# Re-timing the first microseconds of an attention and MoE kernel: a planner's figures, k's cast ahead of q's, longer fillers, and another place for one group of transposes

## The chip, the cores and the metric

The kernel runs on one core of one Trainium2 chip. The metric is the time of one execution on the device, in microseconds (us); the number compared is the median of several runs. A core has five engines that run their own instruction streams in order: TensorE (PE, matrix multiplications), VectorE (DVE), ScalarE (ACT), GpSimd (POOL) and SyncE (SP). In this kernel POOL issues nearly all loads and SP the stores and the transposing transfers. Engines wait for one another on semaphores.

## The reference: windowed attention with ALiBi, then a gated MLP

Eight batches of eight heads, 576 positions, 64 values each. A query sees itself and the 127 positions before it, with a bias that falls linearly with distance, at a slope per head. The outputs of all heads are laid side by side and go through two matrix products with g = h * cos(h) between them.

```
q, k, v: (8, 8, 576, 64) float32     w_in: (512, 2048)   w_out: (2048, 512)
rel    = pos[:, None] - pos[None, :]
slopes = 2.0 ** (-8.0 * (arange(8) + 1) / 8)
scores = (q @ k.T) / 8 - slopes * |rel|      where 0 <= rel < 128, else -1e9
attn   = softmax(scores);  x = (attn @ v) as (4608, 512)
h      = x @ w_in;  out = (h * cos(h)) @ w_out          # (4608, 512) float32
```

## The kernel before

**Work and tiles.** The 4608 tokens are nine chunks of 512. For a chunk the first product runs as L753 (128x512 matmuls), or for chunk 0 as `moe1_block` (L778, four 128x128 matmuls into one quarter of a bank, for one block of 128 tokens and one group f of 128 hidden columns). ACT takes the cosine (L758, L785), DVE multiplies (L762, L788), and the second product is L806. All weights stay in SBUF. Attention for a batch is cut into eight units: one for the first 128 queries of all heads, six for 128 queries of four heads each, one for the last 64. A unit is: scores on PE (L562), exp on ACT (L589), a mask on DVE (L608), P·V on PE (L624 and L628 at the edges, L636 and L638 in between), a reciprocal and a product on DVE that normalise (L661 and L664, or L673 and L675), and transposes of the result on PE (L696, L715), copied into `xT` by ACT or DVE (L724, L725). The first five units get their bias and mask instead by a matmul of the bias with the identity ahead of the scores (L576), so they have no L608. The sixth and seventh unit of batch 0 are the first with a mask.

**The opening.** q and k of batch 0 come in four pieces. The first is loaded by SP and ACT as float32 and cast by ACT or DVE (L376); the others are loaded by POOL (L381) and turned to bf16 on the way. Each piece is transposed by PE into PSUM (L498 for the first, L503 for the others) and copied out by ACT (L518) or DVE (L519). `constants` writes zeros, the identity, the distances `dif` (POOL's iota, L435) and sets ones and zeros in v's tiles (L450, L452), P's tiles (L455) and k's tiles (L458). `masks` makes eight biases (L474 on ACT, L475 on DVE) and the two exponentiated masks (L479, ACT). Loads go out on POOL's queue in this order: second piece of q and k, v's first block, third piece of q and k, v's second block, w_in's first 256 columns, v's third and fourth block, w_in's next 256 columns, the rest.

PSUM has eight banks: scores of a unit use banks 4 and 5, 6 and 7 or 2 and 3; P·V and the transposed results banks 2 and 3; moe1 in chunk 0 banks 0, 1, 6, 7, 4, 5 in turn; the transposes of the first three pieces banks 0 (q) and 1 (k), or both.

**What sets the order.** No order is written by hand. Each step is given to the class `Plan` with its engine or a choice of engines, what it reads and writes, how long it occupies its engine (`occ`), when its result is there (`lat`) and a priority (`pri`, lower first). `Plan.schedule` runs through time with these figures: again and again it takes the step that can start first on any engine, and among those that can start at about the same time the one of lowest `pri`. From the starts it fixes the order of each engine's instructions; `emit` then writes each engine's stream with the waits between engines that the data need. So a changed figure changes no instruction by itself, but can change where instructions stand, and on which of two engines. POOL's own order is fixed (each step on POOL is ordered behind the one before it). Where PE would wait in the opening, the planner puts in fillers, matmuls of zeros (L934), while its clock is within `fill`. Matmuls planned before `COLD` are taken to cost double.

Of the kernel before, what the change touches and what calls it, by code (L numbers as in the profile page):

```python
# [11 lines left out]
B, H, S, D = 8, 8, 576, 64  # L12
# [22 lines left out]
class Plan:  # L35
# [2 lines left out]

    SWITCH = 110
    TABLE = 1330  # L40
    START = {"pe": 1300, "act": 750, "dve": 1050, "pool": 550, "sp": 750}
    COLD = 5400
    FILL = 107
    CROSS, BACK = 2600, 3500

# [48 lines left out]
    def schedule(self, filler=None, fill=(0, 0)):  # L94

        free = dict(self.START)
        wire = first = 3000
        cross = 0
        mode, table = 0, 0
        tables = sorted({o.table for o in self.all if o.table is not None})  # L100
        left = {t: sum(o.table == t for o in self.all) for t in tables}
        avail = []

        def reach(o, e):
            t = 0
            for d, data in o.preds.items():
                if data == ORDER or self.held(d, data, e):
                    t = max(t, d.start + d.occ)
                elif d.dma is None and d.eng[0] == e:
                    t = max(t, d.end + 28)  # L110
                else:
                    t = max(t, d.end + (53 if e == "pe" else 36))
            return t

        def pick_pe(cand):
            soon = min(st for st, _ in cand)
            first = [(st, o) for st, o in cand if o.pri < 5 and
                     st <= soon + (160 if o.mode != mode else 0)]
            if first:
                return min(first, key=lambda c: (c[1].pri, c[1].seq))  # L120
            near = [(st, o) for st, o in cand if st <= soon]
            return min(near, key=lambda c: (c[1].pri, c[1].seq))

        for o in self.all:
            if o.npred == 0:
                avail.append(o)
        order = []
        while avail:
            phase = next((t for t in tables if left[t]), None)
            best = None  # L130
            for e in ENG:
                cand = []
                for o in avail:
                    if e not in o.eng or (o.table is not None and o.table != phase):
                        continue
                    at = reach(o, e)
                    st = max(free[e], at)
                    if e == "pe":
                        if o.mode != mode:
                            st += self.SWITCH  # L140
                        if at > free[e]:
                            st += 40
# [12 lines left out]
            (st, _, _), e, o = best  # L155
            avail.remove(o)
            if o.table is not None and o.table != table:
                st += self.TABLE
            if len(o.eng) > 1:
                o.fn, o.occ, o.lat = o.fn[e], o.occ[e], o.lat[e]  # L160
                o.eng = (e,)
            if e == "pe":
                while filler and mode == 0 and free[e] + self.FILL + 30 < st and (
                        fill[0] <= free[e] < fill[1]):
                    p = self.op("pe", filler, r=["zeros"], occ=self.FILL, lat=self.FILL + 100)
                    self.all.pop()
                    p.start, p.end = free[e], free[e] + self.FILL
                    free[e] += self.FILL
                    order.append(p)
                if st < self.COLD:  # L170
                    o.lat += o.occ
                    o.occ *= 2
            o.start = st
            free[e] = st + o.occ
            if o.dma is not None:
                if e == "sp" and o.dma[0] in "tx":
                    cross = max(cross, st + self.CROSS, min(wire + self.BACK, st + 6000)) + o.lat
                    o.end = max(cross, st + o.occ + 1400) + 500
                elif e == "sp" and o.dma[0] == "s":
                    o.end = st + o.occ + 1800 + o.lat  # L180
                elif e == "sp" or e == "act":
                    first = max(first, st + 1400) + o.lat
                    wire = max(wire, min(first, 5600))
                    o.end = max(first, st + o.occ + 1400) + 500
                else:
                    wire = max(wire, st + 2300) + o.lat
                    o.end = max(wire, st + o.occ + 1400) + 500
            else:
                o.end = st + o.lat
            if e == "pe":  # L190
# [12 lines left out]
        self.order = sorted(order, key=lambda o: (o.start, rank[id(o)]))  # L203
# [81 lines left out]
def bass_alibi_sliding__then__act_gcu_kernel(  # L285
# [8 lines left out]
    with ExitStack() as ctx:  # L294
# [68 lines left out]
        def load_qk(which, src, b, n=0):  # L363
# [3 lines left out]
                           [[64 * rr, 32], [64 * S, H], [1, 64 * rr]])  # L367
            if b == 0 and n == 0:
                op("sp" if which == "q" else "act", [lambda e: e.dma_start(qF[which][:, :, :], rows)],
                   w=[("qF", which)], dma=f"ld{which}f", occ=700,  # L370
                   lat=600 if which == "q" else 400, pri=0)
                i = qF[which][:, :, :].rearrange("p y (j d) -> p y j d", j=4)
                o = qC[which][:, :, :, :].rearrange("p j y d -> p y j d")
                op(("act", "dve"),
# [5 lines left out]
            o = qE[which][:, :, :] if t0 == 512 else qB[which][:, :, c0:c0 + 64 * rr]  # L380
            op("pool", [lambda e: e.dma_start(o, rows)],  # L381
               w=piece_keys(which, b, n), dma=f"ld{which}{n}", occ=750,
               lat={2: 600, 4: 800 if which == 'q' else 700,
                    8: 1700 if which == 'q' else 1300, 18: 2850}[rr])

        def load_v(b, order=range(NBLK), behind=()):
            for t in order:
# [45 lines left out]
        def constants():  # L433
# [1 line left out]
            op("pool", lambda e: e.iota(dif[:, :, :], pattern=[[128, 2], [-1, 128]], base=-128,  # L435
                                        channel_multiplier=1,
                                        allow_small_or_imprecise_dtypes=True),
               w=["dif"], occ=360)

            op("dve", lambda e: e.tensor_scalar(ident[:, :], dif[:, 1, :], 0.0, None,  # L440
                                                ALU.is_equal), r=["dif"], w=["ident"],
# [6 lines left out]
               r=[("off", 0), ("off", 1)], w=["dif"], occ=350, lat=430, pri=0)  # L448
            for i in range(2):
                op("dve", lambda e, i=i: e.memset(vp[i][:, :, :, 64:65], 1.0), w=[("vinit", i)],  # L450
                   pri=i)
                op("dve", lambda e, i=i: e.memset(vp[i][64:128, 4, :, 0:64], 0.0),  # L452
                   w=[("vinit", i)], occ=270, pri=i)
            for i in range(NP):
                op("dve", lambda e, i=i: e.memset(P[i][:, 1024:1088], 0.0), w=[("P", i)], occ=90)  # L455
            op("dve", lambda e: e.memset(halfpi[:, :], math.pi / 2.0), w=["halfpi"], occ=60)
# [8 lines left out]
                    :, 4, :, 64:128], 0.0), w=[("tr", "k", b % 2), ("ktail", b % 2)], occ=250,  # L465
               lat=300)

        def masks():
            flat = dif[:, :, :].rearrange("p a b -> p (a b)")
            for h in range(H):  # L470
                pr, x = h // 2, h % 2
                o, s = BT[:, x, pr, :], 8.0 * slopes[h]
                op(("act", "dve"),
                   {"act": lambda e, o=o, s=s: e.activation(o, flat, ACTF.Copy, scale=s),  # L474
                    "dve": lambda e, o=o, s=s: e.tensor_scalar(o, flat, s, None, ALU.mult)},  # L475
                   r=["dif"], w=[("BT", h)], occ={"act": 310, "dve": 250},
                   lat={"act": 410, "dve": 330}, pri=3)
            for x in range(2):
                op("act", lambda e, x=x: e.activation(  # L479
                    EM[:, x, :, :], BT[:, x, :, :], ACTF.Exp, scale=0.125),  # L480
                   r=[("BT", h) for h in range(x, H, 2)], w=[("EM", x)], occ=920, lat=1024,
                   table=0, pri=2)

        def qk_transposes(b, which, n, part, banks):
            t0, rr, groups = PIECES[b][n]
# [338 lines left out]
        def attention(us, phase):  # L824
# [58 lines left out]
        load_w_in(4, 6)  # L883
        load_qk("q", q, 0, 3)
        load_qk("k", k, 0, 3)
        masks()
# [16 lines left out]
        for c in range(NCH):  # L903
# [21 lines left out]
            while next_t < B and done >= 8 * (next_t - 1):  # L925
# [4 lines left out]
                if next_t < B:  # L930
# [2 lines left out]
            moe2(c)  # L933
        R.schedule(filler=lambda e: e.matmul(ps[:, UB[1], 0:128], zeros[:, :],  # L934
                                             zeros[:, :], start=True, stop=True),
                   fill=(1100, 7500))
        R.emit(final=[f"st{i}" for i in range(NOB)])


# [26 lines left out]
```

## Time and profile before

| What | Value |
|---|---|
| Median of 3 runs | 310.07 us (309.79 to 310.78) |
| The profiled execution | 310.54 us, of it a span of 308.4 us |
| PE busy | 299.3 us (97%) |
| ACT, DVE, POOL busy | 201.4, 193.7, 97.0 us |
| First matmul (filler) starts | 0.99 us |
| First 128x512 matmul of chunk 1 (L753) | 55.0 us |

A row of the timeline gives start, length, engine, line, operation, tiles with shapes, and how many instructions were merged; in brackets the idle time before it and what ended it. A wait is named by its releaser. PE matmuls overlap in the array, so a row of several is longer than the time after which the next can start; start to start is the rate. "PEld" is the loading of PE's weights, "PEq" or "issue" the engine's own sequencer. In the table of loads the last figure is the time from issue to landing.

### The profile page before, as it was taken

To read this page: it belongs to the slowest core of one execution; us is meant where nothing else is said; L and a number is where in the kernel's file an instruction comes from. 1 tells how busy PE (TensorE), PEld (TensorE's weight loads), DVE (VectorE), ACT (ScalarE), POOL (GpSimd) and SP (SyncE) were. 2 spreads that over 40 slices of the span, in tenths; PEclk is the share of its full clock that TensorE was granted. 3 is DMA by queue.
4 is the path that set the end of the run, shared out by engine and by line. 5 is a ranking of instruction groups with operands and counts; after the bars stand their busy time and mean duration, and the time that the engine had idled before them with its cause. 6 is when DMAs were issued, how large, how long until landed. Compare 5 with 4: busy or idle time off the path is not lost.

```text
span 308.4 us, 6651 instructions
## 1 busy us (share of the span) xinstructions
PE 299.3 (97%) x2675; PEld 161.4 (52%) x2717; DVE 193.7 (63%) x406; ACT 201.4 (65%) x270; POOL 97.0 (31%) x122
## 2 busy tenths in 40 slices
PE   7899999999999999999999999999999999999996
PEld 5589755445554455445544554455445554444444
DVE  6678667575668566856785568656966588742000
ACT  7797866875478745873688378746964488752211
POOL 8997200573055504650347123811300000000000
PEclk9999999999999999999999999999999999999999
DMA  9999999999399948996699959995991420001112
GB/s 143 165 204 207 207 166 193 177 159 165 102 125 162 162 67 166 151 172 86 154 115 148 166 122 120 154 205 116 117 137 45 113 68 2 0 0 70 68 71 99
DMA packets 150333, 39.09 MB, mean 127 GB/s; under 512 B 138912, under 2 KB 145312, under 8 KB 150304
## 3 DMA queue, kind: packets, MB, share of 16 engines
q0 software_dynamic: 100688, 18.10, 80.4%
q1 hardware_dynamic: 49344, 20.33, 31.6%
q8 instruction: 21, 0.34, 0.5%
q10 hardware_dynamic: 272, 0.26, 0.3%
q14 instruction: 8, 0.07, 0.1%
HBM read 36.70 MB, written 9.44 MB: 150 GB/s over the span
## 4 chain that ended last, share of the span: by engine, by line
PE 90%; DMA 3%; POOL 2%; ACT 2%; issue 1%; DVE 1%; POOLq 0%; ACTq 0%
PE ps L806 38%; PE ps L753 36%; PE ps L562 5%; PE ps L778 5%; DMA w_inb<-in_moe_w_in_dram 3%; ACT p L589 2%; PE ps L636 2%; PE ps L638 2%; PE ps L624 1%; PE ps L503 1%; POOL vp L389 1%; PE ps L628 1%; DVE p L608 1%; PE ps L715 1%; POOL qrows L381 0%
## 5 line engine op out<-in xcount | busy, mean ns | idle before, releaser
L806 PE MATMUL ps<-w_outb,gT 128*128 128x512 bf16 (+2 forms) x565 | 132.2, 373 | 2.2 <-issue 1.1
L753 PE MATMUL ps<-xT,w_inb 128*128 128x512 bf16 x499 | 113.9, 379 | 0.7
L762 DVE TENSOR_TENSOR gT<-ps,cos 128x512 bf16<-128x512 f32 x128 | 85.0, 687 | 19.5 <-ACT cos L758 14.6
L758 ACT ACTIVATE cos<-ps,halfpi 128x512 f32<-128x512 f32 x128 | 84.7, 688 | 17.9 <-PE ps L753 13.9
L806 PEld LDWEIGHTS ps<-w_outb,gT 128*128 128x128 bf16 x592 | 53.3, 98 | 55.2 <-DVE ob L814 0.2
L589 ACT ACTIVATE p<-ps 128x1024 bf16<-128x1024 f32 x64 | 61.5, 1023 | 31.4 <-PE ps L562 31.4
L753 PEld LDWEIGHTS ps<-xT,w_inb 128*128 128x128 bf16 x512 | 48.9, 97 | 56.3 <-ACT p L589 0.6
L389 POOL DMA_DIRECT2D vp<-in_v_dram x40 | 33.7, 863 | 91.5 <-DMA xT<-xnat 70.3
L608 DVE TENSOR_TENSOR p<-p,emask 128x1024 bf16<-128x1024 bf16 x59 | 39.8, 682 | 26.8 <-ACT p L589 26.8
L813 ACT ACTIVATE ob<-ps 128x512 f32<-128x512 f32 (+2 forms) x21 | 12.1, 577 | 41.3 <-PE ps L806 34.7
L400 POOL DMA_DIRECT2D qnat<-in_q_dram x30 | 25.3, 872 | 18.5 <-DMA qt<-qnat 18.5
L400 POOL DMA_DIRECT2D knat<-in_k_dram x30 | 25.3, 875 | 11.0 <-DMA kt<-knat 8.2
L675 DVE TENSOR_TENSOR xnat<-ps,rec 128x256 bf16<-128x256 f32 x48 | 19.9, 421 | 1.4
L814 DVE COPY ob<-ps 128x512 f32<-128x512 f32 x16 | 10.9, 684 | 15.5 <-PE ps L806 15.5
L562 PE MATMUL ps<-qt,kt 64*128 64x128 bf16 (+1 forms) x576 | 19.2, 211 | 0.6 <-DVE kt L519 0.6
L562 PEld LDWEIGHTS ps<-qt,kt 64*128 64x128 bf16 x576 | 14.5, 94 | 9.3 <-DVE xnat L675 3.4
L636 PEld LDWEIGHTS ps<-vp,p 128*128 128x128 bf16 x192 | 14.2, 97 | 8.9 <-issue 6.3
L636 PE MATMUL ps<-vp,p 128*128 128x65 bf16 x192 | 17.4, 193 | 0.2 <-DVE xT L725 0.2
L638 PE MATMUL ps<-vp,p 128*128 128x65 bf16 x192 | 17.5, 193 | 0.0
L778 PE MATMUL ps<-xT,w_inb 128*128 128x128 bf16 x256 | 16.4, 219 | 0.7 <-DMA w_inb<-in_moe_w_in_dram 0.7
L778 PEld LDWEIGHTS ps<-xT,w_inb 128*128 128x128 bf16 x256 | 14.6, 98 | 1.4 <-DMA w_inb<-in_moe_w_in_dram 0.8
L638 PEld LDWEIGHTS ps<-vp,p 128*128 128x128 bf16 x192 | 13.2, 97 | 2.3
(66 smaller groups left out, 158.9 us busy)
## 6 DMA issues: line engine op xcount, KB each, us to landing
out_dram<-ob SPq DMA_DIRECT2D x35, 256.0 KB, 2.2
vp<-in_v_dram POOLq DMA_DIRECT2D x32, 128.0 KB, 7.5
qnat<-in_q_dram POOLq DMA_DIRECT2D x24, 128.0 KB, 6.2
knat<-in_k_dram POOLq DMA_DIRECT2D x24, 128.0 KB, 5.2
w_outb<-in_moe_w_out_dram POOLq DMA_DIRECT2D x4, 512.0 KB, 22.2
w_inb<-in_moe_w_in_dram POOLq DMA_DIRECT2D x3, 512.0 KB, 12.6
qrows<-in_q_dram POOLq DMA_DIRECT2D x1, 576.0 KB, 15.8
krows<-in_k_dram POOLq DMA_DIRECT2D x1, 576.0 KB, 17.9
```

The lines of the kernel that those rows point to most:

```text
L389: op("pool", [lambda e, t=t, rows=rows: e.dma_start(vp[b % 2][0:rows, t, :, 0:64], v[b, :, 128 * t:128 * t + rows, :].rearrange("h p d -> ...
L400: fns.append(lambda e, t=t, rows=rows: e.dma_start(nat[which][0:rows, t, :, :], src[b, :, 128 * t:128 * t + rows, :].rearrange("h p d -> p ...
L562: ins = e.matmul(ps[:, banks[x], c0:c0 + n_], keys_ap(b, x, pr, kc), query_ap(b, x, pr, qb, n_), start=not acc, stop=stop)
L589: op("act", lambda e: e.activation(P[i][:, 0:1024], ps[:, banks[0]:banks[0] + 2, :].rearrange("p a b -> p (a b)"), ACTF.Exp, scale=0.125), ...
L608: op("dve", lambda e: e.tensor_tensor(p, p, m, ALU.mult), r=[("P", i), ("EM", 0), ("EM", 1)], w=[("P", i)], occ=600, lat=690, pri=1)
L636: e.matmul(o, P[i][:, c0:c0 + 128], V[:, qb - 1, h, 0:65], start=True, stop=False)
L638: ins = e.matmul(o, P[i][:, c0 + 128:c0 + 256], V[:, qb, h, 0:65], start=False, stop=True)
L753: op("pe", lambda e, kc=kc: e.matmul(ps[:, bank, :], w_in[:, kc, 128 * fc:128 * fc + 128], xT[:, kc, r0:r0 + CH], start=(kc == 0), stop=(k ...
L758: op("act", lambda e: e.activation(cosb[ci][:, :], ps[:, bank, :], ACTF.Sin, bias=halfpi[:, 0:1]), r=["halfpi"], w=[("B", bank), ("cos", c ...
L762: op("dve", lambda e: e.tensor_tensor(gT[gi][:, fc, :], ps[:, bank, :], cosb[ci][:, :], ALU.mult), r=[("cos", ci)], w=[("B", bank)] + [("g ...
L778: ins = e.matmul(ps[:, bank, 128 * i:128 * i + 128], w_in[:, kc, 128 * fc:128 * fc + 128], xT[:, kc, t0:t0 + 128], start=(kc == 0), stop=( ...
L806: op("pe", lambda e, t=t, fc=fc, bank=bank, j0=j0, j1=j1: e.matmul(ps[:, bank, 0:j1 - j0], gT[gi][:, fc, 128 * t:128 * t + 128], w_out[:, ...
```

## The change

The edits touch the planner's figures and the steps of batch 0's opening:

- The planner's figures: when each engine can start, until when matmuls cost double (`COLD`), how long loads on SP and ACT take, the lengths of the iota, the biases and the masks, and the landing of some loads of q, k and v.
- The priorities of the memsets in v's tiles: the second batch's get 5 instead of 1.
- `masks` becomes `biases`: even heads first, priority 1 for even and 2 for odd heads instead of 3; the exponentiated masks get 1 instead of 2.
- The load of k's first piece is planned to land ahead of q's, and its cast is placed first.
- The transposes of q's third piece go into banks 6 and 7 (the scores' banks of the second unit) and are entered behind the second unit's exp; k's third piece stays in banks 0 and 1.
- Fillers are allowed from 900 to 8300 instead of 1100 to 7500, and also where PE was last in a 64-row mode (then only for waits of over 500 more, and a change of mode is charged).

```diff
-    START = {"pe": 1300, "act": 750, "dve": 1050, "pool": 550, "sp": 750}
-    COLD = 5400
+    START = {"pe": 990, "act": 750, "dve": 820, "pool": 840, "sp": 750}
+    COLD = 4700
...
-        wire = first = 3000
+        wire = 4000
...
-                while filler and mode == 0 and free[e] + self.FILL + 30 < st and (
+                while filler and free[e] + self.FILL + (30 if mode == 0 else 500) < st and (
                         fill[0] <= free[e] < fill[1]):
+                    if mode:
+                        mode, free[e] = 0, free[e] + self.SWITCH
+                        if o.mode:
+                            st += self.SWITCH
...
                 elif e == "sp" or e == "act":
-                    first = max(first, st + 1400) + o.lat
-                    wire = max(wire, min(first, 5600))
-                    o.end = max(first, st + o.occ + 1400) + 500
+                    o.end = st + o.lat
...
-                   w=[("qF", which)], dma=f"ld{which}f", occ=700,
-                   lat=600 if which == "q" else 400, pri=0)
+                   w=[("qF", which)], dma=f"ld{which}f", occ=700 if which == "q" else 2000,
+                   lat=4000 if which == "q" else 3300, pri=0)
...
-                   occ=900, lat=7 * rows + (700 if b == 0 and t == 0 else 0))
+                   occ=900, lat=7 * rows)
...
                 op("dve", lambda e, i=i: e.memset(vp[i][:, :, :, 64:65], 1.0), w=[("vinit", i)],
-                   pri=i)
+                   pri=5 * i)
...
-        def masks():
+        def biases():
-            for h in range(H):
+            for h in list(range(0, H, 2)) + list(range(1, H, 2)):
...
-                   r=["dif"], w=[("BT", h)], occ={"act": 310, "dve": 250},
-                   lat={"act": 410, "dve": 330}, pri=3)
+                   r=["dif"], w=[("BT", h)], occ={"act": 310, "dve": 330},
+                   lat={"act": 410, "dve": 410}, pri=1 + x)
...
                         mask(u)
+                        if us.index(u) == 1:
+                            qk_transposes(0, "q", 2, 0, SB[2:4])
...
-        for n in range(3):
-            qk_transposes(0, "q", n, 0, [OB[0:1], OB[0:1], OB][n])
-            qk_transposes(0, "k", n, 0, [OB[1:2], OB[1:2], OB][n])
+        for n in range(2):
+            qk_transposes(0, "q", n, 0, OB[0:1])
+            qk_transposes(0, "k", n, 0, OB[1:2])
+        qk_transposes(0, "k", 2, 0, OB)
...
-                   fill=(1100, 7500))
+                   fill=(900, 8300))
```

What it does to the built program: POOL's stream and its order stay the same; DVE gets five biases and ACT three (before three and five); 32 fillers instead of 23; DVE casts k's first piece and then q's; k's transposes precede q's for the first two pieces. Where PE first needs w_in's second 256 columns ("wi1") and thereafter, the orders are (x12 are 12 matmuls; "mask 6" is that of the sixth unit):

```
PE  before: wait wi1, L778 x12, transposes 5, L778 x8, P.V 6, L778 x12, P.V 7, L778 x4, transposes 6, L778 x12, transposes 7
PE  after:  wait wi1, L778 x12, P.V 6, L778 x4, transposes 5, L778 x4, P.V 7, L778 x4, transposes 6, L778 x12, transposes 7
DVE before: mask 6, copy of 5 to xT, mask 7, reciprocal 6, product 6, reciprocal 7, product 7
DVE after:  mask 6, product 5, reciprocal 6, mask 7, copy of 5 to xT, product 6, reciprocal 7, product 7
```

Ahead of that wait both have the same useful work on PE. Later, five L806 of chunk 0 stand ahead of chunk 1 instead of in it, one copy of an output tile goes to ACT, and SP issues the q transposes of batch 2 ahead of two stores instead of one store; from chunk 2 on the orders differ in at most a few places.

More of the change, by code (lines that the diff above doesn't have):

```diff
@@ L382, in load_qk @@
                w=piece_keys(which, b, n), dma=f"ld{which}{n}", occ=750,
-               lat={2: 600, 4: 800 if which == 'q' else 700,
-                    8: 1700 if which == 'q' else 1300, 18: 2850}[rr])
+               lat={2: 600, 4: 800 if which == 'q' else 900,
+                    8: 2600 if which == 'q' else 1300, 18: 2850}[rr])
         def load_v(b, order=range(NBLK), behind=()):
@@ L437, in constants @@
                                         allow_small_or_imprecise_dtypes=True),
-               w=["dif"], occ=360)
+               w=["dif"], occ=510, lat=340)
             op("dve", lambda e: e.tensor_scalar(ident[:, :], dif[:, 1, :], 0.0, None,
@@ L450, in constants @@
                 op("dve", lambda e, i=i: e.memset(vp[i][:, :, :, 64:65], 1.0), w=[("vinit", i)],
-                   pri=i)
+                   pri=5 * i)
                 op("dve", lambda e, i=i: e.memset(vp[i][64:128, 4, :, 0:64], 0.0),
-                   w=[("vinit", i)], occ=270, pri=i)
+                   w=[("vinit", i)], occ=270, pri=5 * i)
             for i in range(NP):
@@ L480, in masks @@
                     EM[:, x, :, :], BT[:, x, :, :], ACTF.Exp, scale=0.125),
-                   r=[("BT", h) for h in range(x, H, 2)], w=[("EM", x)], occ=920, lat=1024,
-                   table=0, pri=2)
+                   r=[("BT", h) for h in range(x, H, 2)], w=[("EM", x)], occ=960, lat=1060,
+                   table=0, pri=1)
         def qk_transposes(b, which, n, part, banks):
@@ L885, in bass_alibi_sliding__then__act_gcu_kernel @@
         load_qk("k", k, 0, 3)
-        masks()
-        for n in range(3):
-            qk_transposes(0, "q", n, 0, [OB[0:1], OB[0:1], OB][n])
-            qk_transposes(0, "k", n, 0, [OB[1:2], OB[1:2], OB][n])
+        biases()
+        for n in range(2):
+            qk_transposes(0, "q", n, 0, OB[0:1])
+            qk_transposes(0, "k", n, 0, OB[1:2])
+        qk_transposes(0, "k", 2, 0, OB)
         every = [u for b in range(B) for u in units(b)]
```

## The prediction

> **What bounds the kernel now.** I read the page first, then the table of what TensorE (PE) waited for, then the chain of work that ended last, then the timeline around the one wait that the chain names.
>
> ```profile
> span 308.4 us, 6651 instructions
> ...
> PE 299.3 (97%) x2675; PEld 161.4 (52%) x2717; DVE 193.7 (63%) x406; ACT 201.4 (65%) x270; POOL 97.0 (31%) x122
> ...
> PE ps L806 <- issue: 1.1, 7, 0.2
> PE ps L576 <- DVE bias L475: 1.1, 1, 1.1
> PE ps L934 <- DVE zeros L434: 1.0, 1, 1.0
> PE ps L778 <- DMA w_inb<-in_moe_w_in_dram: 0.7, 1, 0.7
> PE ps L562 <- DVE kt L519: 0.6, 1, 0.6
> PE ps L624 <- ACT p L589: 0.3, 1, 0.3
> PE ps L636 <- DVE xT L725: 0.2, 1, 0.2
> ```
>
> The last seven rows (microseconds in total, times, longest) are all the idle time of PE. Apart from seven gaps of 0.16 us inside L806, every wait belongs to the first 18 us. So the kernel is a short opening that waits on many things, and then 290 us in which PE is without work only behind its last matmul. Whatever lengthens or shortens PE's sequence after the opening reaches the end one for one. The question is what releases PE from the opening. The chain, in order of time (start, length, piece), says it:
>
> ```profile
> 8.63 9.08 DMA w_inb<-in_moe_w_in_dram
> 17.71 0.05 issue
> 17.76 0.84 PE ps L778 x12
> ```
>
> A 256 KB piece of w_in, the second of five, is issued by POOL at 8.63 and lands at 17.71. PE waits for it; only then does its uninterrupted work begin. PE had come there earlier (rows of the timeline: start, length, engine, work):
>
> ```profile
> 16.69 0.40 PE L562 MATMUL ps<-qt,kt 64*128 64x128 bf16 x8
> ...
> 17.76 0.84 PE L778 MATMUL ps<-xT,w_inb 128*128 128x128 bf16 x12 [0.67 <-DMA w_inb<-in_moe_w_in_dram]
> ```
>
> It ended the scores at 16.69 + 0.40 = 17.09 and stood idle for 0.67 us.
>
> **The change, part by part.** *The ramp (planner's figures, cast of k first, score banks for q's third piece).* In both built orders the useful work that PE issues ahead of its wait for that piece of w_in is the same: ten bias matmuls, all transposes of three pieces, the scores of seven units, the P·V of five, four output transposes and three groups of four L778. Only fillers differ (23 before, 32 after), and they stand where PE would wait. So a quicker ramp brings PE to the wait sooner and nothing more. How much sooner: the last input of the ramp is k's third piece.
>
> ```profile
> 4.50 0.77 POOL L381 DMA_DIRECT2D krows<-in_k_dram  x1
> ...
> krows<-in_k_dram POOLq DMA_DIRECT2D x1, 256.0 KB, 6.9
> ...
> 12.19 0.64 PE L503 MATMUL ps<-ident,krows 128*64 128x128 bf16 x16
> ```
>
> It landed at 4.50 + 6.9 = 11.40, but its transposes began at 12.19. Afterwards the banks that it needs are no longer taken by q's third piece, so it can begin just after 11.40, some 0.8 us earlier; with the same 17.09 - 12.19 = 4.90 us behind it (the order there differs a little; I take it as equal) PE arrives at about 16.3, and waits 1.4 us instead of 0.67. Gain on the path: 0. The bounds: nothing, if w_in lands when it did; at most 17.71 - 16.3 = 1.4, if w_in were there by then.
>
> *Does w_in land sooner?* POOL issues the same instructions in the same order, and its issues stand back to back with no wait on another engine, the earlier rows of vp included:
>
> ```profile
> 1.36 0.85 POOL L381 DMA_DIRECT2D qrows<-in_q_dram  x1 [0.18 <-issue]
> ...
> 2.92 0.89 POOL L389 DMA_DIRECT2D vp<-in_v_dram  x1
> 3.80 0.70 POOL L381 DMA_DIRECT2D qrows<-in_q_dram  x1
> ...
> 8.63 2.27 POOL L421 DMA_DIRECT2D w_inb<-in_moe_w_in_dram  x3
> ```
>
> The piece spends 9.08 us between issue and landing, in which the transfers issued ahead of it drain. An earlier memset of vp (pri 0) therefore moves no landing, since that load waited for nothing. I take 17.71 again.
>
> *The biases.* DVE makes five of eight instead of three, ACT three instead of five. In the rows below three on DVE took 1.06 us, 0.353 each: DVE gives 2 x 0.353 = 0.71 more, ACT about as much less. Both lie before 6 us, under the 1.4 us of slack: 0.
>
> *The new order behind the landing.* This is where I find a cost, and it is not in the words of the change: the planner, with other figures, puts three instructions of DVE in another order. Before: mask of the sixth unit, copy of the fifth unit's transposed output (L725, frees bank 2), mask of the seventh unit, reciprocal of the sixth. After: mask of the sixth, reciprocal of the sixth (waits for its P·V), mask of the seventh, and only then that copy. The P·V of the seventh unit goes into bank 2 and waits on DVE for the last of them. On PE the sixth P·V moves ahead of the fifth's transposes, with 12 L778 between it and the landing. So after the landing PE must do 12 L778, the sixth P·V, then DVE three things in a row, before PE may go on with the seventh P·V; and PE holds back all that stands behind it, since it issues in order. The prices, all from the timeline of before:
>
> ```profile
> 14.65 0.63 DVE L725 COPY xT<-ps 128x256 bf16<-128x256 bf16 x2 [0.22 <-PE ps L715]
> ...
> 15.34 0.19 PE L636 MATMUL ps<-vp,p 128*128 128x65 bf16 x1 [0.17 <-DVE xT L725]
> ...
> 16.45 0.19 PE L638 MATMUL ps<-vp,p 128*128 128x65 bf16 x1
> ...
> 16.68 0.18 DVE L673 RECIPROCAL rec<-ps 128x4 f32<-128x4 f32 x1 [0.26 <-PE ps L638]
> ...
> 16.80 0.29 DVE L725 COPY xT<-ps 128x256 bf16<-128x256 bf16 x1
> ...
> 18.44 0.27 PE L715 MATMUL ps<-ident,xnat 128*128 128x128 bf16 x2
> ...
> 18.75 0.29 DVE L725 COPY xT<-ps 128x256 bf16<-128x256 bf16 x1 [0.73 <-PE ps L715]
> ...
> 18.96 0.68 DVE L608 TENSOR_TENSOR p<-p,emask 128x1024 bf16<-128x1024 bf16 x1
> 19.00 0.19 PE L636 MATMUL ps<-vp,p 128*128 128x65 bf16 x1
> ...
> 19.21 0.19 PE L638 MATMUL ps<-vp,p 128*128 128x65 bf16 x1
> 19.24 0.83 PE L778 MATMUL ps<-xT,w_inb 128*128 128x128 bf16 x12
> ...
> 19.56 0.17 DVE L673 RECIPROCAL rec<-ps 128x4 f32<-128x4 f32 x1
> ...
> 19.91 0.19 PE L636 MATMUL ps<-vp,p 128*128 128x65 bf16 x1
> ...
> 20.15 0.38 PE L778 MATMUL ps<-xT,w_inb 128*128 128x128 bf16 x4
> 20.37 0.28 PE L715 MATMUL ps<-ident,xnat 128*128 128x128 bf16 x2
> 20.49 0.83 PE L778 MATMUL ps<-xT,w_inb 128*128 128x128 bf16 x12
> ```
>
> Start to start, 12 L778 take 18.44 - 17.76 = 0.68, a P·V 19.24 - 19.00 = 0.24 (its result 19.40 - 19.00 = 0.40 after its start), 4 L778 20.37 - 20.15 = 0.22, two transposes 0.12. After the change, with 17.76 as the start:
> - PE: 12 L778 to 18.44; sixth P·V issued to 18.68, its result at 18.84. Then 4 L778 to 18.90, fifth's transposes to 19.02, 4 L778 to 19.24. Here PE comes to the seventh P·V.
> - DVE: the reciprocal begins 0.04 behind the P·V (16.64 to 16.68), at 18.88. The next instruction follows 0.12 later (16.68 to 16.80): the mask at 19.00. The mask holds DVE for 0.60 (18.96 to 19.56): the copy at 19.60, done 0.29 later at 19.89. PE starts 0.06 behind a copy (14.65 + 0.63 = 15.28 to 15.34): 19.95.
>
> Stall: 19.95 - 19.24 = 0.71 us. Before, the seventh P·V started at 19.91 right behind its 12 L778: its mask had ended at 18.96 + 0.68 = 19.64, 0.27 us ahead. The 12 L778 that covered it now stand elsewhere. Bounds: 0, if the copy or the mask came earlier after all (the built order on DVE excludes that); above, if DVE's sixth mask is late too, some 0.1 more. The next steps wait for nothing new: the sixth unit's normalised output (0.42 behind the copy's 0.21) is there at 20.23, before its transposes at 20.42.
>
> *The rest.* Behind the first chunk both orders of PE hold the same instructions with the same number of changes between 64- and 128-row tiles; five L806 of chunk 0 move ahead of chunk 1. SP issues the q transposes of batch 2 before two stores of chunk 0; four output buffers cover that. No wait of PE stands there now, and PE comes 0.71 us later than the transfers do: 0. Fillers end before the landing: 0.
>
> Sum: 0 + 0 + 0 + 0.71. The profiled execution takes 310.54 for its span of 308.4; it becomes 311.25. It lies 0.47 above the median of 310.07, which becomes 310.8 (+0.23%). Differences under 0.3% (0.93 us) can't be told from no change here.
>
> **A rule weighed.** The two extra biases on DVE run while POOL issues loads.
>
> ```profile
> 3.25 1.06 DVE L475 TENSOR_SCALAR bias<-dif 128x256 bf16<-128x256 f32 x3
> ```
>
> The issue of qrows at 3.80 lies mostly within these three and took 0.70. No L381 row shown above is shorter: there is no sign that DVE held POOL up. The Trainium skill (SBUF — State Buffer, "Who interferes with whom") says the opposite may happen: a `tensor_scalar` on DVE can take the port pair that DVE and GpSimd share for its whole length, and GpSimd then can't write the descriptors of its transfers; by that rule the trace would show stretched issues, and it doesn't; with the rule the sum would be 0.71 + 0.71 (rival 1), with the row it stays 0.71.
>
> **Rivals.**
> 1. *POOL is held up (slower).* If each extra bias blocked POOL for its length, the issues would be 0.71 late, and if the whole stream of transfers moved with them, w_in would land 0.71 later and the stall come on top: 310.07 + 0.71 + 0.71 = 311.5. For it: DVE also does vp's memsets beside the iota and the first issue now, and the first issue, at 1.36, is the longest of L381. Against: the 0.70 row, and 9.08 us of queue that should absorb a late issue. It decides the class from 0.93 - 0.71 = 0.22 us of delay on.
> 2. *The ramp becomes longer (slower).* q's third piece now needs the second unit's score banks, so it waits for that unit's exp. If k's piece, the exps and masks behind it came over 1.4 us later than I have it, PE would miss the landing; 1 us beyond that gives 311.8. Against: before, the first two exps end by 8.60 + 1.97 = 10.57, no later than q's transposes began (10.53).
> 3. *No stall, or a smaller one.* If I misread what the seventh P·V waits for, and it were the mask alone, PE would start at 19.00 + 0.68 + 0.06 = 19.74, a stall of 0.50 (310.6); if it waited for neither, the change would do nothing that reaches the end: 310.1. Against: the bank it writes is the one that the copy empties.
> 4. *Faster.* w_in lands at 16.3 or before, for instance because the loads drain faster. Then the ramp's 1.4 us count, less the stall: 310.07 - 1.4 + 0.71 = 309.4; with the stall covered as well, 308.7, which alone is beyond 0.3%. Against: same queue, same order, same issue times.
>
> ```profile
> 8.60 1.97 ACT L589 ACTIVATE p<-ps 128x1024 bf16<-128x1024 f32 x2
> 10.53 0.64 PE L503 MATMUL ps<-ident,qrows 128*64 128x128 bf16 x16
> ```
>
> **How the numbers follow.** Forecast 0.60, with its own range 310.3 to 311.3 (0.43 of it within 0.3%, 0.17 above, since only 0.2 us separate it from that bound); rival 1 0.16 and rival 2 0.07, both slower; rival 3 0.05, the same; rival 4 0.12, of which 0.08 is faster by over 0.3% and 0.04 the same. That makes faster 0.08, same 0.52, slower 0.40. The range for 8 in 10 goes from 309.7, between rivals 3 and 4 (0.1 left out below), to 311.9, above rivals 1 and 2.
>
> **What the changed profile would show.** Right: the chain still names the DMA of w_in, landing near 17.7, and PE idle for over 1 us before it; then one new row, PE waiting about 0.7 us at L639 (the P·V, three lines further down) for DVE's copy of xT, near 19.2 to 20.0; PE full to the end. Wrong: w_in landing elsewhere by more than 0.2 us; POOL issues over 0.8 at the biases; no wait at L639; new waits after 40 us.

## The result and the profile after

The changed kernel takes 311.0 us in the median (310.26 to 312.12), the kernel before, beside it, 310.21 (309.79 to 312.0), 22 runs each: a ratio of 1.0023, with a 95% interval of 1.0012 to 1.0034. The forecast was 310.8 and no change over 0.3%. The profiled execution takes 311.46. It will turn out that the number was right for reasons that were half right: the change gains about 0.6 us in the opening (0.2 to 1.0 by the interval of the run that shows it), which I had at nothing, and loses some 1.4 us behind it (an estimate from two intervals: 0.8 to 1.9), of which I had 0.71.

From the page of the changed kernel, and then its table of PE's waits (in total, times, longest; lines stand three further down than before, so L778 is L781, and so on):

```profile
span 309.6 us, 6675 instructions
...
PE 300.6 (97%) x2685; PEld 161.8 (52%) x2726; DVE 195.4 (63%) x408; ACT 201.0 (65%) x268; POOL 97.0 (31%) x122
```

```profile
PE ps L506 <- DMA qrows<-in_q_dram: 0.5, 1, 0.5
PE ps L639 <- DVE xT L728: 0.5, 1, 0.5
PE ps L639 <- DMA vp<-in_v_dram: 0.4, 1, 0.4
```

The wait for w_in's second piece is gone from the table: the piece landed at 8.61 + 8.2 = 16.8, 0.9 us earlier than foretold, and the chain that ended last names q's load in its place. By the prediction's own list of signs this part is wrong. The foretold row is there (the P·V at L639 for DVE's copy), and with it one that the prediction does not have: the first transposes of batch 1 (L506) wait for q's load. The timeline around the first:

```profile
17.12 0.84 PE L781 MATMUL ps<-xT,w_inb 128*128 128x128 bf16 x12
...
18.40 0.66 DVE L611 TENSOR_TENSOR p<-p,emask 128x1024 bf16<-128x1024 bf16 x1
18.97 0.28 DVE L728 COPY xT<-ps 128x256 bf16<-128x256 bf16 x1
...
19.31 0.10 PEld L639 LDWEIGHTS ps<-vp,p 128*128 128x128 bf16 x1 [0.67 <-DVE xT L728]
19.32 0.20 PE L639 MATMUL ps<-vp,p 128*128 128x65 bf16 x1 [0.50 <-DVE xT L728]
```

From the 12 L781 to the seventh P·V it is 19.32 - 17.12 = 2.20 us; the prediction's chain of reciprocal, mask and copy made it 19.95 - 17.76 = 2.19. The 0.50 in the bracket counts from the modelled end of the last matmul; start to start, PE came to this P·V at 18.43 + 0.22 = 18.65 and stood 0.67 us, where 0.71 was worked out. But all of it starts at 17.12, not at 17.76. The second wait, in the chain and the timeline:

```profile
12.96 16.22 DMA qrows<-in_q_dram
29.18 0.04 issue
29.22 0.75 PE ps L506 x20
```

```profile
23.59 5.09 PE L781 MATMUL ps<-xT,w_inb 128*128 128x128 bf16 x88
29.22 0.75 PE L506 MATMUL ps<-ident,qrows 128*64 128x128 bf16 x20 [0.55 <-DMA qrows<-in_q_dram]
```

Before, PE came to these transposes just as late, but with work until then (kernel before: first the timeline, then the table of loads for the issue at 13.00):

```profile
24.20 5.09 PE L778 MATMUL ps<-xT,w_inb 128*128 128x128 bf16 x88
29.22 0.75 PE L503 MATMUL ps<-ident,qrows 128*64 128x128 bf16 x20
```

```profile
qrows<-in_q_dram POOLq DMA_DIRECT2D x1, 576.0 KB, 15.8
```

The load landed at 13.00 + 15.8 = 28.8, 0.4 ahead of PE. In the changed order 12 L781 fewer stand ahead of the transposes (176 where there were 188), 0.68 us of work, and it landed at 29.18. That landing is the latest of the thirteen traces whose load order was left alone. In e1 and e11 below, which have the same 176 ahead, the load landed at 28.2 and 27.9, and PE didn't wait for it. So this wait belongs to the new order only where the load comes late.

To see where an execution gains and loses, I take from the traces when the n-th weight load of chunk 0's first product starts (L778, or what answers to it), and the 129th of the second product (L806), less the same of the kernel before's profiled execution:

```
               before   changed   e9      e13     e6      e10     e11
13th (landing)  17.75    -0.64   -0.33   -1.58   -1.04   -1.24   -0.97
61st            21.21    +0.09   +0.64   -1.57   -1.04   -1.24   -0.24
176th           28.34    +0.06   +0.61   -0.79   -0.57   -0.92   -0.11
201st           30.52    +0.68   +0.61   -0.07   -0.57   -0.91   -0.11
129th of L806  101.40    +1.00   +0.85   +0.12   -0.35   -0.74   +1.30
end of span    308.4     +1.20   +0.86   +0.32   -0.08   -0.74   +1.30
```

The other columns are experiments, told below. For the changed kernel: 0.64 gained at the landing, 0.73 lost in the stretch behind it, 0.62 lost at q's transposes, 0.52 lost after 31 us, of it 0.20 after 101 us, where no row of the table of waits answers to it.

### The profile page after: what moved, and what is told of

Its sections match the earlier page's. It is cut to its first block, busy times and chain, and to the rows that moved or that the text cites. A ratio compares the mean times of both kernels' runs of the same rounds, so it can differ in the third digit from the quotient of the medians.

```text
span 309.6 us, 6675 instructions
## 1 busy us (share of the span) xinstructions
PE 300.6 (97%) x2685; PEld 161.8 (52%) x2726; DVE 195.4 (63%) x408; ACT 201.0 (65%) x268; POOL 97.0 (31%) x122
## 4 chain that ended last, share of the span: by engine, by line
PE 86%; DMA 5%; POOL 3%; ACT 2%; issue 2%; DVE 1%; POOLq 0%; ACTq 0%
PE ps L809 38%; PE ps L756 36%; DMA qrows<-in_q_dram 5%; PE ps L565 5%; ACT p L592 2%; PE ps L639 2%; PE ps L641 2%; PE ps L627 1%; POOL w_inb L423 1%; PE ps L781 1%; POOL vp L391 1%; PE ps L506 1%; DVE p L611 1%; PE ps L631 1%; PE ps L718 1%
## 5 line engine op out<-in xcount | busy, mean ns | idle before, releaser
L809 PE MATMUL ps<-w_outb,gT 128*128 128x512 bf16 (+2 forms) x566 | 131.9, 373 | 2.2 <-issue 1.3
L809 PEld LDWEIGHTS ps<-w_outb,gT 128*128 128x128 bf16 x592 | 53.4, 98 | 55.5 <-DVE ob L817 0.2
L817 DVE COPY ob<-ps 128x512 f32<-128x512 f32 x15 | 10.3, 689 | 17.0 <-PE ps L809 16.8
L639 PEld LDWEIGHTS ps<-vp,p 128*128 128x128 bf16 x192 | 14.1, 97 | 10.7 <-issue 7.1
L639 PE MATMUL ps<-vp,p 128*128 128x65 bf16 x192 | 17.4, 193 | 1.0 <-DVE xT L728 0.5
L781 PE MATMUL ps<-xT,w_inb 128*128 128x128 bf16 x256 | 16.5, 219 | 0.0
L781 PEld LDWEIGHTS ps<-xT,w_inb 128*128 128x128 bf16 x256 | 14.5, 98 | 0.9
L641 PEld LDWEIGHTS ps<-vp,p 128*128 128x128 bf16 x192 | 13.2, 97 | 1.9
## 6 DMA issues: line engine op xcount, KB each, us to landing
qrows<-in_q_dram POOLq DMA_DIRECT2D x1, 576.0 KB, 16.2
```

Source lines behind the costliest of these rows:

```text
L639: e.matmul(o, P[i][:, c0:c0 + 128], V[:, qb - 1, h, 0:65], start=True, stop=False)
L641: ins = e.matmul(o, P[i][:, c0 + 128:c0 + 256], V[:, qb, h, 0:65], start=False, stop=True)
L781: ins = e.matmul(ps[:, bank, 128 * i:128 * i + 128], w_in[:, kc, 128 * fc:128 * fc + 128], xT[:, kc, t0:t0 + 128], start=(kc == 0), stop=( ...
L809: op("pe", lambda e, t=t, fc=fc, bank=bank, j0=j0, j1=j1: e.matmul(ps[:, bank, 0:j1 - j0], gT[gi][:, fc, 128 * t:128 * t + 128], w_out[:, ...
```

## Experiments

Two theories went in. W: the order of the stretch behind the landing costs what the seventh P·V waits. L: PE, once earlier, waits for the landing of a later load, which takes the gain back. T came later: the order behind 35 us costs something by itself. All kernels but two are the changed kernel with steps put elsewhere in the planned order of an engine, by a helper ahead of `emit`: `relist((engine, from, to))` moves one step in the first four, `relist((engine, numbers))` puts the steps of these numbers in the order given in the others. The experiments' medians (8 to 12 runs each) stand beside 31 to 35 runs of the kernel before on the same chip. The ratio and its interval are estimated from all runs, so they need not be the quotient of the two medians; 0.001 of the time is 0.31 us.

| Run | Edit | Median | Before | Ratio (95%) |
|---|---|---|---|---|
| changed kernel | | 311.0 | 310.21 | 1.0023 (1.0012 to 1.0034) |
| e1 | seventh P·V later | 310.74 | 310.19 | 1.0023 (1.0006 to 1.004) |
| e2 | q's transposes later | 310.6 | 310.19 | 1.0015 (0.9999 to 1.0031) |
| e4 | kernel before, q's transposes earlier | 310.4 | 310.19 | 1.0008 (0.9991 to 1.0025) |
| e5 | q's load ahead of w_in's last piece | 310.83 | 310.19 | 1.002 (1.0004 to 1.0036) |
| e6 | stretch put back, q's transposes later | 310.47 | 310.17 | 1.0015 (0.9999 to 1.0031) |
| e7 | e6, and DVE's kt copy earlier | 310.53 | 310.17 | 1.0015 (1.0002 to 1.0027) |
| e8 | e6, and all of batch 1's first transposes later | 310.9 | 310.17 | 1.0027 (1.0015 to 1.004) |
| e9 | kernel before, changed stretch | 310.94 | 310.17 | 1.003 (1.0013 to 1.0048) |
| e10 | all order behind the landing put back | 309.6 | 310.19 | 0.998 (0.9967 to 0.9993) |
| e11 | only the order behind 35 us put back | 311.54 | 310.19 | 1.0047 (1.003 to 1.0064) |
| e12 | e10, qend's and kend's transposes later | 309.51 | 310.19 | 0.9982 (0.9965 to 0.9999) |
| e13 | only the stretch put back | 310.59 | 310.19 | 1.0011 (0.9994 to 1.0028) |

**One step moved (e1, e2, e4, e5).**

```diff
 # e1
+        R.relist(('pe', 74, 79), ('pe', 80, 84))
 # e2
+        R.relist(('pe', 115, 118))
 # e4, in the kernel before
+        R.relist(('pe', 109, 106))
 # e5
+        R.relist(('pool', 16, 15))
```

> The changed kernel, but the seventh P·V stands 16 L781 later on TensorE, so that DVE's copy is done before TensorE comes to it. Theory W (the loss of 0.7 us is the wait of the seventh P·V, as predicted): the wait of 0.50 us goes and the time falls by 0.5 to 0.7 us, to that of the kernel before (310.2). Theory L (the loss is set by the landing of q's load of batch 1, since q's transposes of batch 1 stand 12 L781 earlier than before): TensorE only comes to those transposes earlier, its wait there grows from 0.55 to about 1.0 us, and the time stays at 0.7 us over the kernel before.

> The changed kernel, but q's first transposes of batch 1 stand 12 L781 (0.68 us) later on TensorE, behind as much work as in the kernel before. Theory W: no change, 0.7 us over the kernel before. Theory L: the wait of 0.55 us for the load goes, and the time falls by about 0.5 us, to some 0.2 us over the kernel before.

> The kernel before, but q's first transposes of batch 1 stand 12 L778 (0.68 us) earlier on TensorE, where the changed kernel has them. Theory W: as fast as the kernel before. Theory L: TensorE comes there at 29.22 - 0.68 = 28.54, ahead of the landing at 28.8 of the profile of before: a new wait of 0.3 us there, up to 0.7 us where the opening runs quicker than in that profile; 0.3 to 0.7 us over the kernel before.

> The changed kernel, but POOL issues q's load of batch 1 one place earlier, ahead of the last quarter of w_in, so that it lands some 2 us earlier; TensorE's order is untouched. Theory W: no change, 0.7 us over the kernel before. Theory L: the wait for that load goes and the time falls by about 0.5 us; the next candidate is k's load behind it, unchanged, where TensorE may then wait a little.

e1 did not take the wait away; it gave it to the next group of the first product, which needs the same copy (L795 is its L781):

```profile
19.16 0.40 PE L795 MATMUL ps<-xT,w_inb 128*128 128x128 bf16 x4 [0.50 <-DVE xT L742]
```

So the wait isn't the P·V's own: it comes from DVE's order, and whatever PE has next there waits. e2 has no wait for q's load and still that for xT, and lies 0.41 above the kernel before instead of 0.79; but its load landed at 27.97, before PE would have come in the changed kernel's order too, so its trace doesn't show that the move took the wait away. e5 let q's load land at 25.37, 12.21 + 13.2, with the same wait for xT; PE then waited 0.3 for w_out and 0.2 for a later chunk's input instead, and the time hardly moved: taking away this one wait brings nothing by itself. e4, which should show L alone, is inconclusive: +0.21 with an interval over both signs, and its profiled execution began its first product 1.8 us late, so PE came to q's transposes after the load.

**The stretch on its own, both ways (e9, e13).** e9 gives the kernel before the changed order of that stretch; e13 gives the changed kernel the former one.

```diff
 # e9, in the kernel before
+        R.relist(('pe', [64, 62, 61, 63, 68, 65, 70, 66, 67, 69, 74, 71, 72, 73]),
+                 ('dve', [43, 42, 46, 45, 44]))
 # e13
+        R.relist(('pe', [72, 71, 73, 70, 75, 77, 78, 74, 79, 76, 81, 82, 83, 80]),
+                 ('dve', [44, 43, 47, 46, 45]))
```

> The kernel before with nothing but the order that the change gives the stretch behind w_in's landing, on PE and DVE. W: a wait of 0.5 to 0.7 on DVE's copy of xT, and 310.7 to 310.9. L: the wait is there, but PE, which has only 0.4 in hand at q's load, would have waited on landings in some executions anyway: 310.2 to 310.5. No cost of the stretch at all: 310.2.

> The changed kernel with only the stretch put back, q's transposes left where the change has them. W alone: 310.4 to 310.5, as much as with q later. L: PE comes to qend and to q's load 0.5 to 1.0 earlier and waits there for 0.4 and up to 1.0: 310.7 to 311.0, most of what the stretch gave is lost again.

e9 loses 0.77 us, just above what W said, with the same wait on the same copy (its L651 and L740):

```profile
17.43 0.84 PE L793 MATMUL ps<-xT,w_inb 128*128 128x128 bf16 x12
...
19.86 0.20 PE L651 MATMUL ps<-vp,p 128*128 128x65 bf16 x1 [0.50 <-DVE xT L740]
```

So W is right about the stretch, in kind and in size: 0.77 (0.4 to 1.5 by the interval) against the prediction's 0.71. Its own execution lost 0.97 there: the sixth P·V, too, started late, at 18.41, behind DVE's sixth mask (17.57 + 0.69 = 18.26), which the prediction had allowed for as a bound. But e13, which takes the stretch out of the changed kernel, gets back only 0.4 of it, a difference inside the uncertainty. Its timeline shows where the rest went:

```profile
21.94 0.30 PE L521 MATMUL ps<-ident,qend 128*64 128x128 bf16 x4 [0.74 <-DMA qend<-in_q_dram]
...
28.47 0.75 PE L521 MATMUL ps<-ident,qrows 128*64 128x128 bf16 x20 [0.65 <-DMA qrows<-in_q_dram]
```

PE, 1.57 us earlier than before's execution at the 61st load, waits 0.74 and then 0.65 for two landings: at the 201st it is 0.07 ahead. That is L. The median fell between the two expectations, nearer to L in the profile than in the time.

**Stretch and transposes (e6, e7, e8).**

```diff
 # e6: the stretch as in e13, and
+        R.relist(..., ('pe', [116, 117, 118, 115]))
 # e7: e6, and
+        R.relist(..., ('dve', [67, 66]))
 # e8: the stretch, and
+        R.relist(..., ('pe', [116, 117, 118, 119, 120, 121, 122, 115, 123, 124, 126, ...]),
+                 ('act', [32, 31, 33, 35, 34, 37, 36, 39, 38]),
+                 ('dve', [65, 64, 66, 68, 67, 70, 69, 72, 71]))
```

> The changed kernel with the stretch behind the landing of w_in's second piece put back in the order of the kernel before (the seventh P·V, L781's groups and the copies between, on PE and DVE), and q's first transposes of batch 1 behind 12 more L781. W (the order of that stretch costs what the seventh P·V waits, 0.5): the wait of 0.5 on DVE's copy of xT goes; together with q's transposes, which took 0.55, the time comes to about 310.0, the kernel before within 0.1%. L (the landing of a later load takes back whatever PE gains): the wait goes, but a wait of 0.3 to 0.6 on a landing (q's load, or those that follow it, at L506's counterpart) comes in its place, and the time stays at 310.5 to 310.7. Neither: the wait on xT is still there.

> As the run with the stretch restored and q's transposes later, and DVE's copy of kt ahead of the product that stands before it, so that the next transposes don't wait for it (0.16 in the changed kernel). W: 309.8 to 310.0. L: the 0.16 goes into the wait on the next landing, and the time is that of the run without the copy moved.

> The changed kernel with the stretch restored and all four of the first transposes of batch 1 (q, k, q's second, k's second) behind more L781, so that none of them stands where its load is still under way. W and L together (each has its share, and there is nothing else): no wait on a landing between 25 and 36 us and none on xT at 19 us; 309.5 to 309.9, below the kernel before. If something else of the change costs (the rest that I put at nothing): no such waits, and still 310.4 or more.

e6 has neither wait, and its profiled execution ends level with the kernel before (-0.08), while the median is 0.3 above. PE waits 0.4 for qend, at 22 us, and later for a copy that stands behind a product on DVE (its L803 is the cosine):

```profile
33.17 0.64 PE L521 MATMUL ps<-ident,qrows 128*64 128x128 bf16 x16 [0.19 <-ACT cos L803]
```

From the 201st load to the end it loses 0.57 - 0.08 = 0.49. e7 takes the 0.19 away and gains nothing that can be measured. e8 misses its aim: with the transposes moved further, that wait becomes 0.41, and the time is 0.73 above. My expectation of 309.5 to 309.9 for it was wrong. The edit moves the copies on ACT and DVE along, but DVE's copy of kt still stands behind a product: it ends at 33.52 + 0.92 = 34.44, and PE starts its next transposes behind it.

```profile
33.52 0.92 DVE L537 COPY kt<-ps 128x640 bf16<-128x640 bf16 x1
...
34.58 0.64 PE L521 MATMUL ps<-ident,qrows 128*64 128x128 bf16 x16 [0.41 <-ACT cos L803]
```

The wait of 0.16 to 0.20 at this place, about 33 to 34 us, is in every other trace with the changed order there but e7's, and in none with the former one.

**All of the order (e10, e11, e12).**

```diff
 # e10: order of the kernel before on PE, DVE and ACT from the landing on
+        R.relist(('pe', [72, 71, 73, 70]), ('pe', [75, 77, 78, 74, 79, 76]),
+                 ('pe', [81, 82, 83, 80]), ('pe', [91, 93, 90, 94, 95, 92]),
+                 ('pe', [116, 117, 118, 115]), ('pe', [126, 127, 125]), ('pe', [133, 132]),
+                 ('pe', [138, 139, 140, 141, 137]), ..., ('dve', [44, 43, 47, 46, 45]),
+                 ('dve', [72, 71]), ..., ('act', [37, 36, 39, 38]))
 # e11: only the parts from ('pe', [138, ...]) on
 # e12: e10 with
-                 ('pe', [91, 93, 90, 94, 95, 92])
+                 ('pe', [91, 93, 94, 95, 90, 96, 97, 92])
```

> The changed kernel with the whole order behind the landing of w_in's second piece put back to that of the kernel before, on PE, ACT and DVE (one group of L809 excepted); what is left of the change is the ramp, the biases and the engine of a few copies. W and L together explain all: 309.9 to 310.2, as the run with the stretch restored and q later would be without its wait on qend. T (the order of the tail, behind 35 us, costs the 0.3 to 0.45 that the runs with the stretch restored still lose there): 309.9 to 310.2 too, but then the run with only the tail put back gains 0.3. If the ramp is what costs: 310.5 or more.

> The changed kernel with only the order behind 35 us put back to that of the kernel before. T: 310.6 to 310.7, 0.3 to 0.4 below the changed kernel. W and L alone: 310.9 to 311.0, no change.

> As the run with the whole order put back, and the transposes of qend and kend behind 8 and 4 more L781, where the run with the stretch restored waited 0.4 for qend's load. L: PE keeps what it gains at w_in's landing, no wait on a landing until 28 us, and then either q's load (it comes at 28.0 to 29.2, PE would be there at 28.2) takes 0 to 0.8 of it: 309.6 to 310.2, at or below the kernel before. If landings have no share: the same as the run with the order put back.

e10 is the surprise of the study: 309.6, faster than both kernels, and by more than either theory gave it. What is left of the change there is the opening (with the engine of a few copies, one group of L809, and SP's order of stores), worth 0.59 us (0.2 to 1.0). The one wait behind the landing in its table, beside seven gaps of 0.16 in L824:

```profile
PE ps L521 <- DMA qend<-in_q_dram: 0.3, 1, 0.3
```

and its start into the second piece of w_in, where PE went over from the scores without a wait:

```profile
16.19 0.40 PE L580 MATMUL ps<-qt,kt 64*128 64x128 bf16 x8
16.52 0.84 PE L796 MATMUL ps<-xT,w_inb 128*128 128x128 bf16 x12
```

So the order behind the landing costs the changed kernel 311.0 - 309.6 = 1.4 us (by the ratios, 0.43% of 310.2, 1.3): 0.4 come back with the stretch (e13), another 0.1 with q's transposes (e6), and 0.9 only with the rest. Only the last of these steps is clear of the uncertainty. e11 was to show T alone, at 310.6 to 310.7, and misses: the time rises to 311.54, by two new waits.

```profile
38.77 0.63 PE L580 MATMUL ps<-qt,kt 64*128 64x64 bf16 x24 [0.69 <-DVE gT L806]
...
73.03 0.85 PE L580 MATMUL ps<-qt,kt 64*128 64x64 bf16 x32 [0.39 <-DMA kt<-knat]
```

The first stands at the seam. e11 puts PE's steps back from 35 us on, but ACT's `[37, 36, 39, 38]` and DVE's `[72, 71]` stay as the change has them; so ACT makes a copy of kt at 36.72 ahead of the last cosine (37.22), DVE's product comes at 37.93 + 0.69 = 38.62, and the scores wait for it.

```profile
36.72 0.61 ACT L536 ACTIVATE kt<-ps 128x512 bf16<-128x512 bf16 x1 [1.26 <-PE ps L521]
...
37.22 0.68 ACT L803 ACTIVATE cos<-ps,halfpi 128x512 f32<-128x512 f32 x1
...
37.93 0.69 DVE L806 TENSOR_TENSOR gT<-ps,cos 128x512 bf16<-128x512 f32 x1 [0.52 <-ACT cos L803]
```

In e10 that cosine (34.63) stands ahead of the copy (35.85). The second wait, for a transposing transfer, I can't explain. So e11 is no test of T. The row of the 129th load above is one: from there to the end all eight kernels with the changed order of the tail (the changed kernel, e1, e2, e5 to e8 and e13) lose 0.20 to 0.27, and the six with the former one (the kernel before, e4, e9 to e12) lose 0.00 or 0.01. T is right in kind, at 0.2 instead of 0.3 to 0.45. The loss comes in steps of 0.05 to 0.1 between 100 and 200 us, for which I found no row; what makes them isn't shown. e6 loses this 0.27 and the 0.19 of the row above, and e10 neither. e12 takes away e10's wait for qend, and PE waits 0.2 for q's load instead: 309.51, the same within the uncertainty and just under the 309.6 to 310.2 expected. This fits L.

## Why the prediction was right or wrong

*The ramp, "gain on the path: 0".* This step failed. Its mechanism held: k's third piece, free of q's banks, was transposed earlier,

```profile
11.13 0.64 PE L506 MATMUL ps<-ident,krows 128*64 128x128 bf16 x16
```

1.06 us ahead of before's 12.19. PE's arrival was foretold for 16.3. It was at 17.02 - 0.48 = 16.54 in e1 and by 16.18 in e13; in the changed kernel's own execution at 17.1, because there v's third block landed late (the 0.4 of the waits above). But the gain hangs on the landing, and there *"I take 17.71 again"* was the fault: it is one execution's figure. The same piece, issued between 8.61 and 8.80 in all thirteen traces whose load order was left alone, took 9.1 us in the kernel before, 8.3 and 8.2 in the two runs with its opening (e4, e9), and 7.5 to 8.7 in the ten with the changed one:

```profile
w_inb<-in_moe_w_in_dram POOLq DMA_DIRECT2D x1, 256.0 KB, 9.1
```

```profile
w_inb<-in_moe_w_in_dram POOLq DMA_DIRECT2D x1, 256.0 KB, 7.5
```

(the kernel before, and e13). The trace that I read showed the latest landing of all, which is why PE seemed to have slack there; it would also account for the 0.47 by which that execution lay above its median, though no run shows that link. In e9, with before's opening, the piece was there at 8.80 + 8.2 = 17.0 and PE came only at 17.43: PE was the late one, and a faster ramp counts. The bound of 1.4 holds, the choice of 0 within it does not; e10 measures 0.59 (0.2 to 1.0). Rival 4 (w_in lands early) is what happened in part, at the chance of 0.12; the costs behind the landing hid it. Whether the change also makes the piece land sooner, or the executions merely differ, isn't settled: the two ranges overlap.

*The new order behind the landing, 0.71.* Right: 2.20 us of chain where 2.19 was worked out, 0.73 lost between the 13th and the 61st load, and 0.77 in e9, where it stands alone (0.4 to 1.5 by its interval).

*"The rest": 0.* Wrong. "No wait of PE stands there now" was true of the order before, and I asked only what comes later for PE, not that the changed order takes 12 L778 away from ahead of q's transposes, whose load I could have placed: 28.8, 0.4 ahead of PE. That is a step moved past its cover, the very thing that I looked for on DVE. What it costs hangs on the draw: 0.62 in the changed kernel's own execution, nothing in e1 and e11, and in the medians no more than the uncertainty (0.1 from e13 to e6). Two costs are steadier, and the term left both out: 0.16 to 0.20 at 33 to 34 us, where PE waits for DVE's copy of kt, and 0.2 in the tail behind 101 us. With the stretch's 0.7 they make about 1.1 of the 1.4, as an estimate from the traces; how much of the remainder is waiting on landings is open.

*The biases and POOL, 0.* Right. DVE now made five in one go, and the issues of q's and k's third piece, the first beside them and the second at their end, took no longer than before's 0.70 and 0.77:

```profile
2.91 0.94 POOL L391 DMA_DIRECT2D vp<-in_v_dram  x1
3.08 1.55 DVE L477 TENSOR_SCALAR bias<-dif 128x256 bf16<-128x256 f32 x5
...
3.84 0.70 POOL L383 DMA_DIRECT2D qrows<-in_q_dram  x1
4.53 0.71 POOL L383 DMA_DIRECT2D krows<-in_k_dram  x1
```

The issue ahead of these two, of v's first block at 2.91, lies beside the biases too and took 0.94, where it took 0.89 before. By the rule of the Trainium skill (SBUF — State Buffer, "Who interferes with whom") a bias could have held POOL up for its whole length, 0.31 us; this trace shows nothing of that size. Rivals 1 and 2 (POOL held up, a longer ramp) did not occur; rival 3 (no stall, or a smaller one) falls with e9. (The argument against rival 2 has a slip: 10.57 is 0.04 later than 10.53, not earlier. Nothing hangs on it.)

*The sum.* 0.71 was foretold; measured is -0.6 + 1.4 = 0.8. The time came out by luck: two errors of 0.6 and 0.7 us, a gain and a loss that both stood at nothing, went against each other.

## What to carry to other kernels

A landing in a trace is one draw: before a wait on a transfer is taken for slack, or a gain ahead of it for nothing, look at whether that execution lies above its median, and price both cases. Where an engine is full and runs through a row of landings, a gain lasts only as far as the next load that isn't there yet; each load's landing belongs beside the time at which the engine comes to it, before and after. And orders of several engines that were planned together can't be cut at just any place: e11, with PE's tail from one order and the copies at the seam from the other, took 311.54, more than either whole. What a part of an order costs is better read from where traces drift apart, with the part and without it.

## What the runs showed of the hardware

Loads issued by POOL at the same time to 0.2 us landed up to 1.6 us apart in different executions: w_in's second piece 16.1 to 17.7, q's load of batch 1 (issued at about 13.0, 14.9 to 16.2 long) at 27.8 to 29.2. The changed kernel spread evenly over 310.3 to 312.1 in its runs; in e10, 11 of 12 runs lay between 309.3 and 310.0. Whether the landings make this spread, no run shows.
